# Top-k attention with two MoE layers on one core: scaling each masked tile on ScalarE in place of the product with v

## The chip, the cores and the metric

The kernel runs on one core of one Trainium2 chip. The metric is the device time of one execution in microseconds (us); lower is better. Engines are named as in the profile: PE is TensorE (matmuls and transposes), DVE is VectorE, ACT is ScalarE, POOL is GpSimd, SP is SyncE, which issues most DMAs.

## The reference

Three stages follow one another. The first is attention over 4 batches, 8 heads, 576 positions and a head size of 64, in which each row keeps only its 32 largest scores:

```python
scores = scale * np.matmul(q, k.transpose(0, 1, 3, 2))
kth = np.partition(scores, -top_k, axis=-1)[..., -top_k:-top_k + 1]
scores = np.where(scores >= kth, scores, -1000000000.0)
attn = np.exp(scores - np.max(scores, axis=-1, keepdims=True))
attn = attn / (np.sum(attn, axis=-1, keepdims=True) + 1e-09)
attn_out = np.matmul(attn, v)
```

The heads are laid side by side to 2304 tokens of 512 numbers. A dense layer follows, `(x @ w_a) * (x @ w_b) @ w_out`, with an inner width of 1536, and then a layer with 8 experts of inner width 1024, in which each token goes to the one expert with its largest gate value.

## The kernel before

**Units and tiles.** Attention goes by units: a batch `b` and a pair of heads `p`, four units to a batch, sixteen in all. The 576 queries of a unit fall into two groups, `g` = 0 with 320 and `g` = 1 with 256. A tile is 128 rows of queries of one head against all 576 keys. Group 0 has four such tiles and a fifth ("M") which holds the last 64 queries of both heads; group 1 has four. So there are nine tiles to a unit and 144 in all. Tiles of kind "N" are handled in pairs, the two heads side by side, and M alone: five steps to a unit, 80 in all.

**One pair.** PE makes the scores in two halves of keys into PSUM (L597 and L601), ACT copies each half to SBUF as `s` (L606), DVE takes elementwise maxima and minima of the halves (L614) and then, by alternating an eight-largest instruction (L625, L641, L644) and a replace instruction (L638), finds the 32nd largest value (L652). ACT computes the exponentials `e` (L633). One DVE instruction a tile (`attn_out`, L680) then compares `s` with the 32nd value, multiplies by `e`, writes the masked tile `am` and adds up its row sum in `r.sum`. PE transposes `am` in blocks of 128 (L706, L715; for M L688 to L691), ACT copies the result to `aT` (L710, L695, L717).

**One group.** When its tiles are done, `attn_av` multiplies the transposed tiles with `v` (L727, L731) and ACT copies the product, transposed and not yet divided by the row sums, to `xc` (L735). `attn_norm` makes the division: POOL adds 1e-9 to the sums (L750), DVE takes reciprocals (L752), ACT spreads each reciprocal over 64 columns in the tile `rr` (L753, L761), PE turns them into rows (L769, and for group 0 L771), and the product is multiplied by them and written to `xf`. In batches 0 and 1 ACT copies the rows to SBUF and POOL multiplies (L776, L777); in batches 2 and 3 DVE multiplies straight from PSUM (L780). POOL also writes a check value (L747).

**What follows.** `moe1(b, ...)` is the dense layer of one batch: ACT rounds `xf` to `xh` (L792), POOL subtracts the rounded part to get `xl` (L794), and PE multiplies with weights that come by DMA (L824, L854), while ACT empties PSUM (L809) and POOL multiplies and splits (L832, L400, L401). The gate of each batch ranks tokens by expert (L956 to L1011), and after the last batch eight expert steps follow (L1182, L1231). In the first quarter of the run ACT, DVE and POOL also unpack weights (L387 to L401).

**What sets the order.** The kernel writes no engine's order by hand. It registers every operation with its engine, a cost, a priority `pos` (small first) and its reads and writes, plays them through a list scheduler, and emits each engine's instructions in the order that comes out. The dense layer has a low priority on PE, so that its matmuls fill what attention leaves free. An engine then runs its own list strictly in that order. Buffers that matter here: two for the pair of masked tiles `am`, one fixed tile for M, one PSUM buffer `tp` for transposes, one PSUM buffer `pv` that the product with v, the transposed fifth block (L715) and the rows of reciprocals share, and two PSUM buffers `ab` for the dense layer.

Of the kernel before, what the change touches and what calls it, by code (L numbers as in the profile page):

```python
# [15 lines left out]
OP = mybir.AluOpType  # L16
# [176 lines left out]
def c_ts(n):  # L193
    return (n / 2 + 66) / 0.96
# [15 lines left out]
def fused_kernel(ctx: ExitStack, tc: tile.TileContext, q, k, v, w_a, w_b, w_out, w_gate, w1, w2, out,  # L210
# [43 lines left out]
    def T(pool, shape, dt, name, bufs):  # L254
        return P_.tile(pool, shape, dt, name, bufs)
# [50 lines left out]
    nc.gpsimd.memset(wg, 0.0)  # L306
    qm_t, rr_t = [], []
    for i in range(2):
        qm_t.append(cst.tile([128, 192], F32R, name=f"qm{i}"))
        nc.gpsimd.memset(fr(qm_t[i]), 0.0)  # L310
    for i in range(opts.get("rr", 1)):
        rr_t.append(cst.tile([128, 5, 128], F32, name=f"rr{i}"))
        nc.gpsimd.memset(rr_t[i], 0.0)
    id2 = cst.tile([128, 64], F32, name="id2")
    nc.vector.tensor_add(id2, idf[:, 0:64], idf[:, 64:128])
    chk_t = cst.tile([128, B * HP * 9], F32, name="chk")
# [12 lines left out]
    QM = [P_.fixed(t) for t in qm_t]  # L329
    RR = [P_.fixed(t) for t in rr_t]  # L330
    AM = [P_.fixed(t) for t in am_t]
# [138 lines left out]
    def prep_unit(u, i, pos, step):  # L470
        u.qm, u.rr = QM[i % 2], RR[i % len(RR)]
        u.qT = T(p_at, [128, 2, 512], F32R, "qT", 2)
# [73 lines left out]
    def new_group(u, g):  # L546
        r = Rec()
        r.u, r.g, r.n, r.nt = u, g, GRP[g][1], len(GT[g]) + 2
        r.kt = T(p_sml, [128, 5, 48], F32, "kt", 2)
        r.sum = T(p_sml, [128, 5], F32, "sum", 2)  # L550
        r.aT = [T(p_at, [128, 4, 320], F32, f"aT{h}", opts.get("aT", 1)) for h in range(2)]
        r.at = T(p_at, [128, 320], F32, "aTt", opts.get("aT", 1))
        r.xc = T(p_at, [128, 320], F32, "xc", opts.get("xc", 1))
        return r
# [99 lines left out]

    def attn_out(i, r, j, kind, h, c, pos, s, e):
        def kth():
            return r.kt()[:, j, 47:48]
        if kind == "M":
            amz, o, ky = AM[0], 0, None
        else:  # L660
            if not h:
                r.am = T(p_at, [128, 2 * S], F32, "am", opts.get("amb", 2))
                r.tp = T(p_ps, [128, 1024], F32, "tp", 1)
            amz, o, ky = r.am, h * S, h

        def am():
            return amz()[:, o:o + S]

        def sc():
            return s()[:, h if kind == "N" else 0]  # L670
        sk = [(s, (h, 0)), (s, (h, 1))]
        amk = (amz, ky)
        if masked(i):
            P(DVE, c_ts(S), pos, lambda: nc.vector.tensor_scalar(am(), sc(), kth(), None, op0=OP.is_ge),
              r=sk + [(r.kt, (j, 5))], w=[amk], label=f"st{i}")
            P(POOL, c_pool(S), pos, lambda: nc.gpsimd.tensor_mul(am(), am(), e()), r=[e], w=[amk])
            P(ACT, c_act(S, True) + 90, pos, lambda: nc.scalar.activation(
                e(), am(), AF.Copy, accum_out=r.sum()[:, j:j + 1]), r=[amk], w=[e, (r.sum, j)])
        else:
            P(DVE, c_dve(S) + 60, pos, lambda: nc.vector.scalar_tensor_tensor(  # L680
                am(), sc(), kth(), e(), op0=OP.is_ge, op1=OP.mult, accum_out=r.sum()[:, j:j + 1]),
              r=sk + [(r.kt, (j, 5)), e], w=[amk, (r.sum, j)], label=f"st{i}")
        if kind == "M":
            tp = T(p_ps, [128, 1024], F32, "tp", 1)
# [34 lines left out]

    def attn_av(r, pos):  # L720
        u, n = r.u, r.n
        pv = T(p_ps, [128, 512], F32, "pv", 1)

        def av():
# [9 lines left out]
          act=7.2 * n / (4 * n + 132))  # L734
        P(ACT, c_act(n), pos - 20, lambda: nc.scalar.copy(r.xc()[:, 0:n], pv()[:, 0:n]), r=[pv], w=[r.xc])  # L735

    def masked(i):

        return any(a <= i < b and i % m < n for a, b, n, m in opts.get("mk", ()))

    def b_norm(b):
        return b in opts.get("pn", (0, 1))

    def attn_norm(i, r, xf, pos):
        u, g, nt = r.u, r.g, r.nt
        c0, n = GRP[g]
        P(POOL, 170, pos, lambda: nc.gpsimd.tensor_sub(  # L747
            chk_t[:, i - nt + 1:i + 1], r.kt()[:, 0:nt, 47], r.kt()[:, 0:nt, 39]),
          r=[r.kt], w=[(CHK, i)])
        P(POOL, 180, pos - 20, lambda: nc.gpsimd.tensor_scalar(r.sum()[:, 0:nt], r.sum()[:, 0:nt], 1e-9, None, op0=OP.add),  # L750
          w=[r.sum])
        P(DVE, 100, pos - 20, lambda: nc.vector.reciprocal(r.sum()[:, 0:nt], r.sum()[:, 0:nt]), w=[r.sum])  # L752
        P(ACT, c_act(256, True), pos - 20, lambda: nc.scalar.copy(  # L753
            u.rr()[:, 2 * g:2 * g + 2, :].rearrange("p i (h d) -> p i h d", h=2),
            r.sum()[:, 0:4].rearrange("p (i h) -> p i h", h=2)[:, :, :, None].to_broadcast([128, 2, 2, 64])),
          r=[r.sum], w=[(u.rr, g)])
        if g == 0:
            def diag():
                for h in range(2):
                    p0 = 64 * h  # L760
                    res = nc.scalar.copy(u.rr()[p0:p0 + 64, 4, p0:p0 + 64],  # L761
                                         r.sum()[p0:p0 + 64, 4:5].to_broadcast([64, 64]))
                return res
            P(ACT, 300, pos - 20, diag, r=[r.sum], w=[(u.rr, 2)])
        rb = T(p_ps, [128, 512], F32, "pv", 1)

        def bc():
            for x in range(2):
                res = nc.tensor.transpose(rb()[:, x * 128:(x + 1) * 128], u.rr()[:, 2 * g + x, :], idf)  # L769
            if g == 0:  # L770
                res = nc.tensor.matmul(rb()[:, 256:320], u.rr()[:, 4, :], id2, start=True, stop=True)  # L771
            return res
        P(PE, 330 - 110 * g, pos, bc, act=0, r=[(u.rr, g)] + ([] if g else [(u.rr, 2)]), w=[rb])
        if b_norm(u.b):
            rs = T(p_at, [128, 320], F32, "rs", 1)
            P(ACT, c_act(n), pos - 20, lambda: nc.scalar.copy(rs()[:, 0:n], rb()[:, 0:n]), r=[rb], w=[rs])  # L776
            P(POOL, c_pool(n), pos, lambda: nc.gpsimd.tensor_mul(xf()[:, u.p, c0:c0 + n], r.xc()[:, 0:n], rs()[:, 0:n]),  # L777
              r=[r.xc, rs], w=[(xf, (u.p, g))], label=f"norm{u.b}{g}")
            return
        P(DVE, c_dve(n), pos - 20, lambda: nc.vector.tensor_mul(xf()[:, u.p, c0:c0 + n], r.xc()[:, 0:n], rb()[:, 0:n]),  # L780
          r=[r.xc, rb], w=[(xf, (u.p, g))], label=f"norm{u.b}{g}")

# [557 lines left out]
    for i, (ui, g, j, groups, b, p, kind, h, c) in enumerate(tiles):  # L1340
# [26 lines left out]
        for x in made:  # L1367
            attn_out(*x)
        pend = []
        if j == R.nt - 1:  # L1370
            attn_av(R, pos + 1)
            attn_norm(i, R, XF[b], pos + 2)
            if p == HP - 1 and g == groups[-1]:
                moe1(b, groups, XF[b], pos + 3)
# [211 lines left out]
```

## Time and profile before

| what | value |
|---|---|
| median of 3 runs | 1232.25 us (1228.04 to 1233.31) |
| the profiled execution, its own time | 1233.15 us |
| its span in the trace | 1231.4 us |
| mean granted TensorE clock | 0.956 of full speed |
| PE busy | 1103.6 us (90%) |
| DVE busy | 896.3 us (73%) |
| ACT busy | 718.1 us (58%) |
| POOL busy | 460.6 us (37%) |

Busy shares are means over stages with different limits, so they are to be read by stage: DVE has nearly all of its work in attention, which ends at about 810 us, PE works to the end. A matmul's end is modelled in the trace, and consecutive matmuls overlap; what one costs is the distance from its start to the next one's. The same goes for DVE and ACT, where the last part of an instruction overlaps with the next. "Idle before" is the time that an engine stood still ahead of an instruction, with what ended it.

### The profile page before, as it was taken

To read this page: it belongs to the slowest core of one execution; us is meant where nothing else is said; L and a number is where in the kernel's file an instruction comes from. 1 tells how busy PE (TensorE), PEld (TensorE's weight loads), DVE (VectorE), ACT (ScalarE), POOL (GpSimd) and SP (SyncE) were. 2 spreads that over 40 slices of the span, in tenths; PEclk is the share of its full clock that TensorE was granted. 3 is DMA by queue.
4 is the path that set the end of the run, shared out by engine and by line. 5 is a ranking of instruction groups with operands and counts; after the bars stand their busy time and mean duration, and the time that the engine had idled before them with its cause. 6 is when DMAs were issued, how large, how long until landed. Compare 5 with 4: busy or idle time off the path is not lost.

```text
span 1231.4 us, 22514 instructions
## 1 busy us (share of the span) xinstructions
PE 1103.6 (90%) x7710; PEld 981.2 (80%) x7710; DVE 896.3 (73%) x2636; ACT 718.1 (58%) x1567; POOL 460.6 (37%) x622
## 2 busy tenths in 40 slices
PE   4656796979999789999999999999999999999996
PEld 2333474868888579889888998989999899999996
DVE  6999999999998999999998999910004545444441
ACT  6667676776667567666765766633224445544551
POOL 3455566755536234234535422455234100000001
PEclk9966798989999999999999999999899999999998
DMA  8487578999677234244243442246535655554450
GB/s 235 130 276 229 164 245 261 323 303 300 208 255 248 93 87 144 109 153 144 78 152 112 132 151 104 86 155 225 191 147 184 189 152 174 176 177 151 159 177 22
DMA packets 116863, 215.49 MB, mean 175 GB/s; under 512 B 28883, under 2 KB 77011, under 8 KB 109061
## 3 DMA queue, kind: packets, MB, share of 16 engines
q1 hardware_dynamic: 113525, 204.52, 52.4%
q0 software_dynamic: 3216, 9.46, 2.0%
q8 instruction: 63, 1.03, 0.4%
q14 instruction: 59, 0.48, 0.1%
HBM read 171.82 MB, written 35.25 MB: 168 GB/s over the span
## 4 chain that ended last, share of the span: by engine, by line
PE 55%; DVE 14%; DMA 11%; issue 8%; ACT 7%; POOL 4%; SPq 1%; POOLq 0%; ACTq 0%; DVEq 0%
PE ab L824 16%; PE ab L854 9%; PE ab L1182 5%; PE pv L727 5%; DVE am L680 3%; DVE m L638 3%; PE ms L1231 3%; PE pv L1231 3%; PE sp L601 3%; DVE kt L641 2%; PE tp L706 2%; DMA xsort<-rows,pi 2%; DMA rawk<-in_k_dram 2%; DMA wt<-wos 1%; PE pv L731 1%
## 5 line engine op out<-in xcount | busy, mean ns | idle before, releaser
L824 PE MATMUL ab<-xh,wt 128*128 128x320 f32 (+1 forms) x1344 | 303.9, 304 | 3.9 <-ACT sb L809 3.8
L824 PEld LDWEIGHTS ab<-xh,wt 128*128 128x128 f32 x1344 | 227.6, 191 | 13.2 <-issue 7.8
L824 PE MATMUL ab<-xl,wt 128*128 128x320 f32 (+1 forms) x672 | 199.9, 297 | 0.0
L638 DVE MATCH_REPLACE8 m<-kt,m 128x288 f32<-128x288 f32 x432 | 188.5, 440 | 0.0
L641 DVE MAX8 kt<-m 128x8 f32<-128x288 f32 x432 | 182.3, 444 | 0.5
L854 PE MATMUL ab<-gH,wt 128*128 128x320 f32 (+1 forms) x768 | 171.8, 305 | 4.5 <-DMA wt<-wos 4.5
L680 DVE SCALAR_TENSOR_TENSOR am<-s,kt,e 128x576 f32<-128x576 f32 x144 | 139.8, 996 | 0.3
L854 PEld LDWEIGHTS ab<-gH,wt 128*128 128x128 f32 x768 | 130.7, 193 | 6.7 <-DMA wt<-wos 3.9
L832 POOL TENSOR_TENSOR sa<-sa,sb 128x320 f32<-128x320 f32 (+1 forms) x96 | 79.6, 829 | 145.0 <-ACT sb L809 144.5
L824 PEld LDWEIGHTS ab<-xl,wt 128*128 128x128 f32 x672 | 128.8, 192 | 0.0
L633 ACT ACTIVATE e<-s,nm 128x576 f32<-128x576 f32 x144 | 108.6, 778 | 11.6 <-POOL nm L628 11.3
L854 PE MATMUL ab<-gT,wt 128*128 128x320 f32 (+1 forms) x384 | 115.1, 300 | 0.0
L1256 POOL DMA_INDIRECT out_dram<-y,ti x23 | 23.0, 999 | 227.6 <-ACT y L1250 212.6
L1100 DVE TENSOR_TENSOR wp<-raw,wp 128x1024 fp32r<-128x1024 f32 (+1 forms) x73 | 67.4, 942 | 55.6 <-ACT wp L1099 55.2
L606 ACT COPY s<-sp 128x576 f32<-128x576 f32 x128 | 81.9, 640 | 42.9 <-PE sp L601 23.7
L706 PE MATMUL tp<-idr,am 128*128 128x128 f32 x512 | 84.8, 304 | 20.3 <-ACT aT L710 7.2
L401 POOL TENSOR_TENSOR gT<-sa,gH 128x320 fp32r<-128x320 f32 (+1 forms) x96 | 84.6, 881 | 45.8 <-ACT gH L400 45.4
L706 PEld LDWEIGHTS tp<-idr,am 128*128 128x128 f32 x512 | 64.1, 155 | 38.6 <-ACT aT L710 15.8
L1182 PE MATMUL ab<-xgh,wp 128*128 128x304 f32 (+6 forms) x352 | 89.4, 312 | 1.1 <-DVE gT L1189 0.7
L710 ACT COPY aT<-tp 128x512 f32<-128x512 f32 x128 | 72.4, 587 | 26.6 <-PE tp L706 25.8
L727 PE MATMUL pv<-aT,vt 128*64 128x320 f32 (+1 forms) x512 | 79.2, 451 | 6.5 <-ACT aT L695 4.5
L809 ACT ACTIVATE sa<-ab 128x320 f32<-128x320 f32 (+1 forms) x120 | 49.4, 412 | 53.9 <-PE ab L824 30.7
(303 smaller groups left out, 2560.8 us busy)
## 6 DMA issues: line engine op xcount, KB each, us to landing
wt<-ws SPq DMA_DIRECT2D x54, 1024.0 KB, 5.6
wt<-wos SPq DMA_DIRECT2D x44, 768.0 KB, 5.7
raw<-in_moe_w_dram SPq DMA_DIRECT2D x64, 512.0 KB, 3.7
kS<-kT SPq DMA_DIRECT2D x24, 304.0 KB, 4.5
xsort<-rows SPq DMA_DIRECT2D x8, 771.0 KB, 14.4
wp<-ws SPq DMA_DIRECT2D x6, 1024.0 KB
vt<-in_v_dram SPq DMA_DIRECT2D x20, 256.0 KB, 3.1
gT<-in_moe_w_a_dram SPq DMA_DIRECT2D x8, 512.0 KB, 4.1
```

The source lines that it names most:

```text
L401: P(POOL, c_pool(cost), pos, lambda: nc.gpsimd.tensor_sub(lo(), src(), fr(hi())), r=rd + wh, w=wl)
L606: P(ACT, c_act(S), pos, lambda hf=hf, sp=sp: nc.scalar.copy(s()[:, :, hf * HS:(hf + 1) * HS], sp()[:, :, 0:HS]), r=[sp], w=[(s, (h, hf)) f ...
L633: P(ACT, c_act(S, True) + 90, pos, lambda h=h, e=e: nc.scalar.activation(e(), s()[:, h], AF.Exp, bias=nm()[:, h], scale=SCALE), r=[(s, (h, ...
L638: P(DVE, c_dve(HS), pos + 5.0 * h, lambda x=x, h=h, j=j: nc.vector.match_replace(out=m()[:, h], in_to_replace=kt(j, 8 * x - 8, 8 * x), in_ ...
L641: P(DVE, c_dve(HS), pos + 5.0 * h, lambda x=x, h=h, j=j: nc.vector.max(out=kt(j, 8 * x, 8 * x + 8), in_=m()[:, h]), r=[(m, h)], w=[KT(j, x)])
L680: P(DVE, c_dve(S) + 60, pos, lambda: nc.vector.scalar_tensor_tensor(am(), sc(), kth(), e(), op0=OP.is_ge, op1=OP.mult, accum_out=r.sum()[: ...
L706: res = nc.tensor.transpose(tp()[:, 512 * h + x * 128:512 * h + (x + 1) * 128], z()[:, 640 * h + x * 128:640 * h + (x + 1) * 128], idf)
L727: nc.tensor.matmul(pv()[64 * h:64 * h + 64, 0:n], u.vt()[:, h, j, :], r.aT[h]()[:, j, 0:n], start=(j == 0), stop=False)
L824: res = nc.tensor.matmul(pa()[:, 0:n], view()[:, m, wi, ko, :], xv()[:, ko], start=(ko == 0 and x == 0), stop=(ko == KO - 1 and x == 2))
L832: P(POOL, c_pool(n), pos, lambda: nc.gpsimd.tensor_mul(sa()[:, 0:n], sa()[:, 0:n], sb()[:, 0:n]), r=[sb], w=[sa])
L854: res = nc.tensor.matmul(pa()[:, 0:n], wv()[:, wi, f, :], gv()[:, f, :], start=(f == 0 and x == 0), stop=(f == HB - 1 and x == 2))
L1182: res = nc.tensor.matmul(pa()[:, 0:cap], p1[ko]()[:, wi, f * 128:(f + 1) * 128], xv()[:, ko], start=(ko == 0 and i == 0), stop=(ko == KO - ...
```

## The change

ACT divides each masked tile by its row sum before the transposes, so that the product with v is already divided. After a pair's (or M's) comparisons, `attn_div` has DVE add 1e-9 to the sums and take reciprocals: two small instructions a step, 80 times each. `attn_out` is split: part 0 is the comparison, part 1 begins with an ACT copy of the 576 columns of `am` in place with the reciprocal as its scale, and goes on with the transposes as before. ACT's copy behind the product with v now writes `xf` and not `xc`. What falls away: the sum on POOL, the reciprocals by group, `rr` and its copies, the turning into rows on PE with its small matrices, the copy of the rows, the products on POOL and DVE. The check value stays. The branch `masked` that is deleted was never taken. No DMA is added, removed or moved.

```diff
+    def attn_div(r, j0, j1, pos):
+        w = [(r.sum, j) for j in range(j0, j1)]
+        P(DVE, 70, pos, lambda: nc.vector.tensor_scalar(r.sum()[:, j0:j1], r.sum()[:, j0:j1], 1e-9, None, op0=OP.add), w=w)
+        P(DVE, 80, pos, lambda: nc.vector.reciprocal(r.sum()[:, j0:j1], r.sum()[:, j0:j1]), w=w)
...
-    def attn_out(i, r, j, kind, h, c, pos, s, e):
+    def attn_out(part, i, r, j, kind, h, c, pos, s, e):
...
-        else:
+        if part == 0:
             P(DVE, c_dve(S) + 60, pos, lambda: nc.vector.scalar_tensor_tensor(
                 am(), sc(), kth(), e(), op0=OP.is_ge, op1=OP.mult, accum_out=r.sum()[:, j:j + 1]),
               r=sk + [(r.kt, (j, 5)), e], w=[amk, (r.sum, j)], label=f"st{i}")
+            return
+        P(ACT, c_act(S, True) + 30, pos, lambda: nc.scalar.activation(
+            am(), am(), AF.Copy, scale=r.sum()[:, j:j + 1]), r=[(r.sum, j)], w=[amk])
...
-        P(ACT, c_act(n), pos - 20, lambda: nc.scalar.copy(r.xc()[:, 0:n], pv()[:, 0:n]), r=[pv], w=[r.xc])
+        P(ACT, c_act(n), pos - 20, lambda: nc.scalar.copy(xf()[:, u.p, c0:c0 + n], pv()[:, 0:n]), r=[pv],
+          w=[(xf, (u.p, r.g))], label=f"norm{u.b}{r.g}")
...
-    def attn_norm(i, r, xf, pos):
+    def attn_check(i, r, pos):
...
-        P(POOL, 180, pos - 20, lambda: nc.gpsimd.tensor_scalar(r.sum()[:, 0:nt], r.sum()[:, 0:nt], 1e-9, None, op0=OP.add),
-          w=[r.sum])
-        P(DVE, 100, pos - 20, lambda: nc.vector.reciprocal(r.sum()[:, 0:nt], r.sum()[:, 0:nt]), w=[r.sum])
...
-        for x in made:
-            attn_out(*x)
+        for x in made:
+            attn_out(0, *x)
+        attn_div(R, j + 1 - len(pend), j + 1, made[-1][6])
+        for x in made:
+            attn_out(1, *x)
```

## Rows read from the trace of the kernel before

**Rows 1.** Busy time in three stretches (us and count, by engine):
```profile
0.00:437.80 437.80, 339.06 (x2154) 265.78 (x2155) 411.25 (x1251) 300.45 (x653) 229.21 (x295) 0.90 0.74 231
437.80:825.40 387.60, 377.98 (x2876) 343.25 (x2874) 342.44 (x1098) 247.78 (x574) 153.84 (x226) 1.00 0.38 123
825.40:1231.40 406.00, 386.54 (x2688) 372.18 (x2684) 142.64 (x288) 169.86 (x340) 77.51 (x103) 0.98 0.50 164
```

**Rows 2.** All engines in order of time, end of batch 1 (start, length, us):
```profile
433.55 0.37 ACT L735 COPY xc<-pv 128x256 f32<-128x256 f32 x1 [1.95 <-PE pv L731]
...
435.31 0.73 POOL L777 TENSOR_TENSOR xf<-xc,rs 128x256 f32<-128x256 f32 x1 [7.03 <-ACT rs L776]
...
437.83 0.35 PE L824 MATMUL ab<-xh,wt 128*128 128x256 f32 x1
```

**Rows 3.** POOL in order of time, end of batch 3's attention:
```profile
812.29 0.74 POOL L794 TENSOR_TENSOR xl<-xf,xh 128x256 fp32r<-128x256 f32 x1 [0.86 <-ACT xh L792]
```

**Rows 4.** PE in order of time, first matmul of batch 3's dense layer:
```profile
825.36 0.41 PE L824 MATMUL ab<-xh,wt 128*128 128x320 f32 x1
```

**Rows 5.** DVE's waits up to 437.8 us (total, times, longest):
```profile
DVE m L614 <- ACT s L606: 7.0, 6, 3.4
DVE sum L752 <- POOL sum L750: 5.1, 6, 2.3
DVE n L614 <- ACT s L606: 3.3, 6, 0.7
```

**Rows 6.** Groups by line (busy us, mean ns | idle before):
```profile
L633 ACT ACTIVATE e<-s,nm 128x576 f32<-128x576 f32 x144 | 108.6, 778 | 11.6 <-POOL nm L628 11.3
...
L1250 ACT ACTIVATE y<-sp,xr 128x512 f32<-128x512 f32 (+6 forms) x19 | 12.4, 683 | 5.7 <-issue 2.6 <-PE sp L1301 1.8 <-PE sp L1273 0.9
...
L1028 ACT COPY rows<-ms 128x512 f32<-128x512 f32 (+1 forms) x16 | 9.4, 586 | 11.3 <-DMA xsort<-rows,pi 10.2 <-PE ms L1025 1.1
...
L753 ACT COPY rr<-sum 128x256 f32<-128x256 f32 x32 | 12.9, 404 | 5.0 <-DVE sum L752 4.8
...
L777 POOL TENSOR_TENSOR xf<-xc,rs 128x320 f32<-128x320 f32 (+1 forms) x16 | 16.0, 999 | 20.3 <-ACT rs L776 20.3
```

**Rows 7.** ACT in order of time, two exponentials back to back:
```profile
452.56 1.44 ACT L633 ACTIVATE e<-s,nm 128x576 f32<-128x576 f32 x2 [0.50 <-POOL nm L628]
```

**Rows 8.** DVE in order of time, small instructions of the gate:
```profile
645.98 0.80 DVE L970 TENSOR_TENSOR gb<-gb,iom 128x40 f32<-128x40 f32 x1
...
647.93 0.19 DVE L998 TENSOR_SCALAR gb<-gb 128x5 f32<-128x5 f32 x1
648.04 0.44 DVE L644 MAX8 kt<-n 128x8 f32<-128x288 f32 x1
648.41 0.16 DVE L1000 RECIPROCAL gb<-gb 128x5 f32<-128x5 f32 x1
648.50 0.71 DVE L614 TENSOR_TENSOR m<-sp,s 128x576 f32<-128x576 f32 x1
```

**Rows 9.** The same instructions with nothing between them:
```profile
932.33 0.17 DVE L998 TENSOR_SCALAR gb<-gb 128x3 f32<-128x3 f32 x1
932.60 0.18 DVE L1000 RECIPROCAL gb<-gb 128x3 f32<-128x3 f32 x1
```

**Rows 10.** POOL in order of time, at the first row of rows 8:
```profile
645.84 0.87 POOL L401 TENSOR_TENSOR gT<-sa,gH 128x320 fp32r<-128x320 f32 x1 [0.89 <-ACT gH L400]
```

**Rows 11.** Instructions of line 389 (shortest, median, longest ns):
```profile
L389 DVE TENSOR_SCALAR gH<-gH x10: 400/410/1522, 10.8 to 223.9; 128x512 int32<-128x512 int32 x10
```

**Rows 12.** DVE busy with line 680 alone, up to 437.8 us:
```profile
0.00:437.80 437.80, 74.46 (x148) 0.90 0.74 231
```

**Rows 13.** PE in order of time, turning reciprocals into rows:
```profile
456.96 0.38 PE L769 MATMUL pv<-idr,rr 128*128 128x128 f32 x2
457.18 0.33 PE L771 MATMUL pv<-id,rr 128*128 128x64 f32 x2
457.32 0.36 PE L824 MATMUL ab<-xh,wt 128*128 128x256 f32 x1
```

More of the change, by code (lines that the diff above doesn't have):

```diff
@@ L306, in fused_kernel @@
     nc.gpsimd.memset(wg, 0.0)
-    qm_t, rr_t = [], []
+    qm_t = []
     for i in range(2):
@@ L310, in fused_kernel @@
         nc.gpsimd.memset(fr(qm_t[i]), 0.0)
[L311 to L315, printed above, removed]
     chk_t = cst.tile([128, B * HP * 9], F32, name="chk")
@@ L329, in fused_kernel @@
     QM = [P_.fixed(t) for t in qm_t]
-    RR = [P_.fixed(t) for t in rr_t]
     AM = [P_.fixed(t) for t in am_t]
@@ L470, in prep_unit @@
     def prep_unit(u, i, pos, step):
-        u.qm, u.rr = QM[i % 2], RR[i % len(RR)]
+        u.qm = QM[i % 2]
         u.qT = T(p_at, [128, 2, 512], F32R, "qT", 2)
@@ L552, in new_group @@
         r.at = T(p_at, [128, 320], F32, "aTt", opts.get("aT", 1))
-        r.xc = T(p_at, [128, 320], F32, "xc", opts.get("xc", 1))
         return r
@@ L660, in attn_out @@
         else:
-            if not h:
+            if part == 0 and not h:
                 r.am = T(p_at, [128, 2 * S], F32, "am", opts.get("amb", 2))
+            if part and not h:
                 r.tp = T(p_ps, [128, 1024], F32, "tp", 1)
@@ L672, in attn_out @@
         amk = (amz, ky)
[L673 to L678, printed above, removed]
-        else:
+        if part == 0:
             P(DVE, c_dve(S) + 60, pos, lambda: nc.vector.scalar_tensor_tensor(
@@ L718, in attn_out, with attn_av @@
               w=[(r.at, o2)], label="aT")
-    def attn_av(r, pos):
-        u, n = r.u, r.n
+    def attn_av(r, xf, pos):
+        u, n, c0 = r.u, r.n, GRP[r.g][0]
         pv = T(p_ps, [128, 512], F32, "pv", 1)
@@ L734, in attn_av @@
           act=7.2 * n / (4 * n + 132))
-        P(ACT, c_act(n), pos - 20, lambda: nc.scalar.copy(r.xc()[:, 0:n], pv()[:, 0:n]), r=[pv], w=[r.xc])
[L737 to L742, printed above, removed]
-    def attn_norm(i, r, xf, pos):
-        u, g, nt = r.u, r.g, r.nt
-        c0, n = GRP[g]
+        P(ACT, c_act(n), pos - 20, lambda: nc.scalar.copy(xf()[:, u.p, c0:c0 + n], pv()[:, 0:n]), r=[pv],
+          w=[(xf, (u.p, r.g))], label=f"norm{u.b}{r.g}")
+    def attn_check(i, r, pos):
+        nt = r.nt
         P(POOL, 170, pos, lambda: nc.gpsimd.tensor_sub(
@@ L749, in attn_norm @@
           r=[r.kt], w=[(CHK, i)])
-        P(POOL, 180, pos - 20, lambda: nc.gpsimd.tensor_scalar(r.sum()[:, 0:nt], r.sum()[:, 0:nt], 1e-9, None, op0=OP.add),
-          w=[r.sum])
-        P(DVE, 100, pos - 20, lambda: nc.vector.reciprocal(r.sum()[:, 0:nt], r.sum()[:, 0:nt]), w=[r.sum])
[L753 to L781, printed above, removed]
     def moe1(b, groups, xf, pos):
@@ L1367, in fused_kernel @@
         for x in made:
-            attn_out(*x)
+            attn_out(0, *x)
+        attn_div(R, j + 1 - len(pend), j + 1, made[-1][6])
+        for x in made:
+            attn_out(1, *x)
         pend = []
         if j == R.nt - 1:
-            attn_av(R, pos + 1)
-            attn_norm(i, R, XF[b], pos + 2)
+            attn_av(R, XF[b], pos + 1)
+            attn_check(i, R, pos + 2)
             if p == HP - 1 and g == groups[-1]:
```

## The prediction

> **What bounds the kernel now.** I looked first at the busy time of each engine, cut where PE takes up a new batch of the dense layer [rows 1]. Up to 437.8 us DVE is busy 411.3 of 437.8 us and PE 339.1. From there to 825.4 PE is busy 378.0 of 387.6 and DVE 342.4; after that PE is busy 386.5 of 406.0 and DVE 142.6. So the first stretch is DVE's and all that follows is PE's.
>
> The second view, all engines in order of time, shows how the two join. The product of batch 1's last group reaches SBUF at 433.55, is multiplied by its reciprocals at 435.31, and PE begins batch 1's dense layer at 437.83 [rows 2]. The end of attention in batches 0 and 1 thus sets when PE gets its long work, and from there PE idles only 9.6 us to 825.4. At the end of batch 3's attention it is the other way round: POOL has the last part of `xl` at 812.29 + 0.74 = 813.0 [rows 3], and PE takes it up at 825.36 [rows 4]. Attention is there 12.3 us early, which hides any loss on DVE behind 437.8 that is smaller than that, and any gain.
>
> The third view, DVE's waits in the first stretch, shows what could be won there: 7.0 + 3.3 us for the score copies of ACT and 5.1 us for POOL's addition to the sums [rows 5].
>
> So the sum has two parts: what DVE needs more or less up to 437.8, and what PE needs more or less after it. What ACT does counts only where it makes one of the two wait.
>
> **The change part by part, up to 437.8 us** (batches 0 and 1: 8 units, 40 steps, 16 groups).
>
> *The two small DVE instructions.* The gate of the dense layer runs the same pair. With another instruction between, the addition is followed after 648.04 - 647.93 = 0.11 us and the reciprocal after 648.50 - 648.41 = 0.09 [rows 8]: 0.20 a step. With nothing between, the reciprocal starts 932.60 - 932.33 = 0.27 us behind the addition [rows 9]; if the addition waits as long for the row sum, the step costs 0.27 + 0.27 + 0.09 = 0.63. Next to the comparison DVE mostly has work of the following pair, so I take 0.20: 40 x 0.20 = **+8.0 us**, up to 40 x 0.63 = 25.
>
> *What leaves DVE.* 16 reciprocals by group at 0.09 are -1.4 us. The wait for POOL's addition goes with it, -5.1 [rows 5]: the addition is DVE's own now. Both together **-6.5**.
>
> *What leaves POOL.* 16 products, 16.0 us [rows 6]. A DVE instruction with two inputs in SBUF stands still while POOL works: 128x40 took 0.80 us at 645.98, and ended with a POOL instruction that ran from 645.84 to 646.71 [rows 8, 10], where a neighbour of a few columns took 0.19. The comparison takes 74.5 of the 437.8 us, 17% [rows 12]; 17% of 16.0 is 2.7 us of overlap, at the mean half of it lost: **-1.4**, between 0 and -2.7.
>
> *Is the new addition held by POOL too?* It has one input in SBUF. With 512 columns such an addition has a median of 410 ns and took up to 1522 [rows 11]; with 5 columns it took 190 ns, but beside a POOL instruction as short as itself [rows 8]. So the bounds are 0 and all additions held. Without its products POOL is busy (229.2 - 16.0) / 437.8 = 49% of the stretch, in instructions of 229.2 / 295 = 0.78 us on average [rows 1]; an addition that comes at any time waits 0.49 x 0.39 = 0.19 us, 40 of them 7.6. I take half, **+3.8**, since the rows lie on either side.
>
> The Trainium skill, "SBUF — State Buffer", section "SBUF: two separate sides", states that VectorE and GpSimd share one pair of ports, held for a whole instruction by whoever comes first, and that on VectorE's side instructions in a two-port mode or with two SBUF inputs take part. The 0.80 us at 645.98 agrees. By the rule, an addition of few columns is held if it runs in that mode, and the term would be 7.6 in place of 3.8; no row here shows which.
>
> *ACT's scaling.* An exponential of the same 576 columns, with one per-partition operand, takes 778 ns; a per-partition scale on another copy lengthens it from 586 to 683 [rows 6], so the scaling should also last 0.78. Two exponentials in a row take 1.44 us [rows 7], so the next instruction starts after 1.44 - 0.78 = 0.66. For the 74 tiles of this stretch that is 49 us. What leaves ACT, 16 spreads of 0.40 = 6.5 us [rows 6] and some smaller copies, I leave at 6.5. ACT goes from 300.5 to 343 us busy, 69% to 78%: no bound, but a fuller queue. Behind a scaling that waits for DVE's reciprocal stand the score copies, and DVE waits for those: 10.3 us now [rows 5]. Idle time on ACT falls from 31% to 22%; if waits rose as 31/22, that would be +4.2. Some of the 8.0 us of new work falls into those very waits, so I take **+2.0**, between -10.3 (all gone, because the group's closing work has left the queue) and +10.
>
> *The step's length.* Before PE can transpose there now stand an addition, a reciprocal and a scaling, 0.20 + 0.78, and 0.66 more for the second head: 1.6 us. At the group's end the way from the product's copy to `xf` shrinks from 435.31 + 0.73 - 433.55 = 2.5 us to that copy itself, 0.37 [rows 2]: 2.1 less. The two nearly cancel where batch 1 ends; I count **0**, -2 to +2. Inside a batch the longer step is covered by the next pair, whose masked tile has a buffer of its own.
>
> Sum to 437.8: 8.0 - 6.5 - 1.4 + 3.8 + 2.0 = **+5.9 us**.
>
> **From 437.8 on.** For group 0, PE gave 457.32 - 456.96 = 0.36 us to the rows, of which the two transposes 0.22 [rows 13]; group 1 has only those. Batches 2 and 3: 8 x 0.36 + 8 x 0.22 = **-4.6 us** on the engine that bounds. Against it, PE's queue now waits for ACT's scaled tile where it waited for DVE's tile. It idles 9.6 us in all in this stretch [rows 1]. Two copies of that sort wait in one queue now, and ACT's busy share goes from 64% to (247.8 + 46 - 6.5) / 387.6 = 74%; I take **+2.0**, from 0 to 14 (below). On DVE, eight units gain and lose as above and lose the products as well; the 12.3 us of lead [rows 3, 4] cover it, and without them 8.0 + 3.8 us would show here too. The stretch behind 825.4 is not touched.
>
> **Total.** 5.9 - 4.6 + 2.0 = +3.3 us on the profiled execution, which took 1233.15 us (span 1231.4, 1.75 around it). The median lies 0.9 below it: 1232.25 + 3.3 = **1235.5**.
>
> **The rivals.** All times stand against the median.
>
> *PE waits for the scaled tile.* For it speaks that PE executes strictly in its list's order, with dense-layer work behind the transposes; against it, that it loses so little now. If each of the 40 steps after 437.8 held PE for half a scaling's distance, 0.35 us, that is 14 in place of 2: 1247.5. It passes 0.5% from about 0.12 us a step. Chance 0.15.
>
> *DVE's small steps stand bare.* If nothing is ready between comparison, addition and reciprocal, the 8.0 becomes 25: 1252.7. Against it speaks that DVE was idle for only 26 us in the first stretch, so work was mostly at hand. Chance 0.06.
>
> *Every addition is held by POOL*, 7.6 for 3.8 (the mechanism of the two-port rule above): 1239.3. Chance 0.10. The skill's page named there gives no more than that condition.
>
> *The group's closing work was what made DVE wait*, the one that ends faster. Before, two copies on ACT, transposes on PE and a product stand at each group's end in the same queues as the next pair's score copies. If the 10.3 us of waits vanish with them, in place of +2.0, the sum is 3.3 - 12.3 = -9.0: 1223.2. For it: these waits are few and long, up to 3.4 us [rows 5], as of something out of the usual beat. Against it: ACT gets seven times more work than it loses. It decides once about 9.5 of the 12.3 are had. Chance 0.20.
>
> **How the numbers follow.** About 0.5% (6.2 us) is what a measurement of this kernel can tell from no change. The forecast's own case, 1229 to 1242, has 0.49; about a sixth of it, 0.08, lies above 1238.4. Slower: 0.15 + 0.06 + 0.10 + 0.08 = 0.39, of which 0.02 stays within since PE's wait may be below 0.12; 0.37. Faster: 0.20, less 0.02 for a partial gain, 0.18. The rest, 0.45, is within 0.5%. The range leaves out the bare steps and the far halves of the PE and closing-work cases, 0.2 in all: 1222 to 1249.
>
> **What the profile after would show.** Up to the start of batch 1's dense layer: line 824 should resume at about 437.8 + 6 = 444 us; if it resumes before 434, the closing-work case holds. Two small DVE instructions 80 times, followed after 0.1 us each; a longest addition near 0.9 us would mean that POOL holds it, below 0.25 that it does not. The scaling near 0.78 us, ACT busy 75 to 80% in attention. No rows from reciprocals on PE. PE idle between the start of batch 1's and of batch 3's dense layer near 12 us; 20 or more speaks for the first rival. Wrong would be the whole frame if PE stood idle behind 825, or if attention's end passed PE's leftover work, so that PE waited for batch 3.

## The result, and the profile after

The changed kernel takes **1248.51 us** (median of 4 runs, 1247.71 to 1251.51) against 1232.78 us for the kernel before in the same comparison: ratio 1.0125, 95% interval 1.0097 to 1.0154, some 15 us slower. The forecast was 1235.5; the measured time lies at the upper end of the range, which ends at 1249. The profiled execution took 1247.71 us, with a span of 1245.7.

The busy times by stretch of the changed kernel, cut at the same two marks as [rows 1] (there 437.8 and 825.4: PE's first dense-layer matmul of batch 1's second group, and of batch 3):

```profile
core 0: us, PE busy (x) PEld busy (x) DVE busy (x) ACT busy (x) POOL busy (x), PEclk, DMA share, GB/s
0.00:467.80 467.80, 348.09 (x2103) 271.13 (x2104) 430.19 (x1324) 332.83 (x676) 206.34 (x262) 0.85 0.69 216
467.80:845.20 377.40, 369.75 (x2829) 336.77 (x2829) 342.64 (x1137) 281.60 (x616) 153.46 (x210) 1.00 0.39 127
845.20:1245.70 400.50, 383.32 (x2688) 368.50 (x2684) 142.57 (x288) 169.48 (x340) 77.36 (x103) 0.99 0.50 166
```

The first stretch is 30.0 us longer, the second 10.2 shorter, the third 5.5 shorter; together +14.3, the difference of the spans. The frame held: DVE sets the first stretch, PE the others. In the first, DVE is busy for 18.9 us more and idle for 11.0 us more (467.8 - 430.2 = 37.6, before 26.6). These two numbers are what has to be explained.

For the busy time, the groups of DVE instructions of the first stretch in the changed kernel, shapes apart (busy, mean ns):

```profile
L674 DVE SCALAR_TENSOR_TENSOR am<-s,kt,e 128x576 f32<-128x576 f32 x74 | 71.9, 991 | 2.0 <-ACT e L626 1.8
L651 DVE TENSOR_SCALAR sum<-sum 128x2 f32<-128x2 f32 x33 | 16.5, 500 | 0.1
L652 DVE RECIPROCAL sum<-sum 128x2 f32<-128x2 f32 x33 | 4.9, 148 | 0.1
L652 DVE RECIPROCAL sum<-sum 128x1 f32<-128x1 f32 x8 | 1.2, 152 | 0.0
L651 DVE TENSOR_SCALAR sum<-sum 128x1 f32<-128x1 f32 x8 | 1.1, 141 | 0.0
```

An addition of one column takes 141 ns, one of two columns 500 on average. The order of time shows why; two of the longest, each beside the POOL instruction under way:

```profile
212.03 1.36 POOL L395 TENSOR_TENSOR gH<-gH 128x512 fp32r<-128x512 f32 x1 [0.73 <-ACT gH L394]
212.18 1.22 DVE L651 TENSOR_SCALAR sum<-sum 128x2 f32<-128x2 f32 x1
...
417.01 1.44 POOL L508 TENSOR_TENSOR hl<-rawq,hl 128x576 fp32r<-128x576 f32 x1 [1.47 <-ACT hl L506]
417.19 1.28 DVE L651 TENSOR_SCALAR sum<-sum 128x2 f32<-128x2 f32 x1
```

POOL ends at 213.39 and 418.45, the additions at 213.40 and 418.47: each stood until POOL was done. Of the 33 additions of two columns in this stretch, 19 began while such a POOL instruction ran and ended 0.02 to 0.03 us behind it; the other 14 took 0.14 to 0.17 us. The addition is held, for a time that has nothing to do with its 256 elements. The Trainium skill has the condition on two pages: "SBUF — State Buffer", section "SBUF: two separate sides", says that a VectorE instruction in a two-port mode waits for a GpSimd instruction that came first, and "VectorE: DVE Perf Modes", section "What auto-detection actually checks", gives as the condition of the mode a single source and the destination in SBUF, with outermost dimensions other than one that are both even or equal. The trace agrees with both: two columns are held, one column is not.

For the idle time, DVE's waits up to 467.8 (us in total, times, longest), to be held against [rows 5]:

```profile
DVE m L607 <- ACT s L599: 14.3, 5, 7.6
DVE gT L383 <- ACT gT L381: 7.2, 1, 7.2
DVE m L607 <- PE sp L594: 5.1, 1, 5.1
DVE n L607 <- ACT s L599: 4.7, 7, 0.8
DVE am L674 <- ACT e L626: 1.8, 2, 1.2
...
DVE m L606 <- ACT s L577: 1.5, 2, 1.1
```

The wait for POOL's sum is gone, and in its place stand longer waits for scores and their copies, most of it in three places: 5.14 us at 244.35, 3.39 at 322.42 and 7.61 at 381.57. All engines in order of time around the longest:

```profile
375.48 0.58 PE L782 MATMUL ab<-xh,wt 128*128 128x256 f32 x1 [3.45 <-DMA wt<-ws]
...
379.70 0.44 PE L594 MATMUL sp<-kT,qT 128*128 128x288 f32 x1
...
380.90 0.64 ACT L599 COPY s<-sp 128x576 f32<-128x576 f32 x1 [1.64 <-PE sp L594]
...
381.57 0.76 DVE L607 TENSOR_TENSOR m<-sp,s 128x576 f32<-128x576 f32 x1 [7.61 <-ACT s L599]
```

No wait for the division is in this chain. PE's list has dense-layer matmuls of batch 0 ahead of the second half of a score. Their weights came late (why was not looked into), PE stood for 3.45 us, and behind the pause it was granted 0.50 of its clock (1.2 GHz) from 375.4 to 380.6; from there to 390 the mean was 0.97. The matmuls in it started 0.21 us apart, not 0.12. Only then came the score, and DVE stood for 7.61 us. That the order of the lists had a part in the loss is what the experiments then had to test, beside the addition and ACT's load.

### The profile page after: what moved, and what is told of

The parts are those of the page before. It is cut to its first block, busy times and chain, and to the rows that moved or that the text cites. A ratio compares the mean times of both kernels' runs of the same rounds, so it can differ in the third digit from the quotient of the medians.

```text
span 1245.7 us, 22374 instructions
## 1 busy us (share of the span) xinstructions
PE 1101.2 (88%) x7614; PEld 976.4 (78%) x7614; DVE 915.4 (73%) x2747; ACT 783.9 (63%) x1631; POOL 437.2 (35%) x573
## 4 chain that ended last, share of the span: by engine, by line
PE 44%; DVE 10%; ACT 7%; issue 7%; DMA 7%; POOL 2%; SPq 0%; POOLq 0%; ACTq 0%; DVEq 0%
PE ab L782 12%; PE ab L812 9%; PE ab L1140 4%; PE ms L1189 3%; PE pv L1189 3%; PE pv L724 2%; DMA xsort<-rows,pi 2%; PE sp L594 2%; PE tp L703 2%; DVE m L631 2%; DVE am L674 2%; DVE kt L634 2%; DMA wt<-wos 1%; ACT am L678 1%; ACT aT L707 1%
## 5 line engine op out<-in xcount | busy, mean ns | idle before, releaser
L790 POOL TENSOR_TENSOR sa<-sa,sb 128x320 f32<-128x320 f32 (+1 forms) x96 | 84.1, 876 | 146.4 <-ACT sb L767 144.2
L678 ACT ACTIVATE am<-am,sum 128x576 f32<-128x576 f32 x144 | 107.4, 773 | 21.8 <-DVE sum L652 21.7
L703 PE MATMUL tp<-idr,am 128*128 128x128 f32 x512 | 81.3, 301 | 27.4 <-ACT am L678 13.0
L703 PEld LDWEIGHTS tp<-idr,am 128*128 128x128 f32 x512 | 64.3, 154 | 43.3 <-ACT am L678 23.7
L724 PE MATMUL pv<-aT,vt 128*64 128x320 f32 (+1 forms) x512 | 80.3, 458 | 4.5 <-ACT aTt L714 2.2
```

The costliest lines, as they stand in the source:

```text
L678: P(ACT, c_act(S, True) + 30, pos, lambda: nc.scalar.activation(am(), am(), AF.Copy, scale=r.sum()[:, j:j + 1]), r=[(r.sum, j)], w=[amk])
L703: res = nc.tensor.transpose(tp()[:, 512 * h + x * 128:512 * h + (x + 1) * 128], z()[:, 640 * h + x * 128:640 * h + (x + 1) * 128], idf)
L724: nc.tensor.matmul(pv()[64 * h:64 * h + 64, 0:n], u.vt()[:, h, j, :], r.aT[h]()[:, j, 0:n], start=(j == 0), stop=False)
L790: P(POOL, c_pool(n), pos, lambda: nc.gpsimd.tensor_mul(sa()[:, 0:n], sa()[:, 0:n], sb()[:, 0:n]), r=[sb], w=[sa])
```

## The experiments

The marks are the two of the table of stretches; "idle" is DVE's idle time in the first. Ratios stand against the kernel before, measured beside each kernel, with their 95% interval. Stretches and idle times are those of the one profiled execution, which lies up to 3.3 us off the median of its kernel (e1 3.1 us above, e3 3.3 below); differences of a few us between two kernels' stretches are therefore not shown by them alone.

| kernel | median us | ratio | first, second, third stretch | idle |
|---|---|---|---|---|
| before | 1232.25 | 1 | 437.8, 387.6, 406.0 | 26.6 |
| changed | 1248.51 | 1.0125 (1.0097 to 1.0154) | 467.8, 377.4, 400.5 | 37.6 |
| e1, no addition | 1237.6 | 1.0040 (1.0020 to 1.0060) | 457.1, 376.1, 405.8 | 41.0 |
| e2, addition by column | 1238.74 | 1.0051 (1.0029 to 1.0074) | 458.1, 376.3, 405.1 | 39.4 |
| e3, no scaling | 1229.76 | 0.9986 (0.9968 to 1.0004) | 446.8, 371.7, 405.9 | 23.7 |
| e4, no division | 1226.8 | 0.9956 (0.9937 to 0.9976) | 444.6, 371.5, 406.3 | 34.5 |
| e10, scaled aside, no addition | 1235.02 | 1.0013 (0.9997 to 1.0030) | 449.0, 375.8, 407.1 | 36.3 |
| e11, one column scaled, no addition | 1225.32 | 0.9927 (0.9905 to 0.9950) | 445.4, 370.7, 407.2 | 34.3 |
| e7, no division, own lists | 1216.21 | 0.9860 (0.9834 to 0.9886) | 435.9, 370.4, 406.3 | 29.3 |
| e12, no addition, own lists | 1220.8 | 0.9886 (0.9863 to 0.9910) | 440.5, 373.9, 404.8 | 28.3 |
| e14, before in other lists | 1232.25 | 0.9998 (0.9979 to 1.0016) | 440.6, 385.9, 406.3 | 30.6 |
| e6, before without POOL's addition | 1230.59 | 0.9980 (0.9963 to 0.9997) | 435.0, 387.6, 403.8 | 22.5 |
| e9, both ways in one | 1215.16 | 0.9852 (0.9831 to 0.9873) | 437.2, 372.5, 404.6 | 24.8 |
| e13, the division in e7's lists | 1318.88 | 1.0682 (1.0650 to 1.0713) | 484.0, 428.1, 405.3 | 67.0 |

In e1 to e4, e6, e10 and e11 an operation keeps its place in the scheduler but issues something else or nothing, so that every engine's order stays as it was.

**e1: the addition left out, same lists.**

```diff
-        P(DVE, 70, pos, lambda: nc.vector.tensor_scalar(r.sum()[:, j0:j1], ...), w=w)
+        P(DVE, 70, pos, lambda: None, w=w)
```

> The changed kernel without the addition of 1e-9 (left out; reciprocal, scaling and the order of everything else stay). Theory A, POOL holds the addition: its 64 instances of two columns last 0.38 us on average, 17.6 us of DVE's time in the first stretch, and DVE bounds that stretch. Then batch 1's dense layer resumes near 468 - 16 = 452 us and the time falls to 1231 to 1237. Theory B, ACT's fuller queue sets the pace (DVE's waits for score copies rose by some 11 us) and the addition stands in waits that are there anyway: the dense layer resumes at 463 or later, 1244 to 1248.

The time fell by 0.85%, some 10.5 us, and the dense layer resumed at 457.1: between the two theories, nearer to A. DVE is busy for 14.1 us less in the stretch (416.1 for 430.2), but idle for 3.4 more, since the three long waits stay:

```profile
234.62 0.76 DVE L607 TENSOR_TENSOR m<-sp,s 128x576 f32<-128x576 f32 x1 [4.08 <-PE sp L594]
...
313.89 0.76 DVE L607 TENSOR_TENSOR m<-sp,s 128x576 f32<-128x576 f32 x1 [3.70 <-ACT s L599]
...
373.35 0.76 DVE L607 TENSOR_TENSOR m<-sp,s 128x576 f32<-128x576 f32 x1 [8.57 <-ACT s L599]
```

**e2: the same additions, column by column.**

```diff
-    lambda: nc.vector.tensor_scalar(r.sum()[:, j0:j1], r.sum()[:, j0:j1], 1e-9, None, op0=OP.add)
+    lambda: [nc.vector.tensor_scalar(r.sum()[:, x:x + 1], r.sum()[:, x:x + 1], 1e-9, None, op0=OP.add)
+             for x in range(j0, j1)][-1]
```

> The changed kernel with each addition of two columns issued as two additions of one column; nothing is left out. In the changed kernel's trace none of the 16 additions of one column lasted over 0.17 us. Theory A, the hold by POOL comes with the second column: 144 additions of about 0.14 us, none over 0.25; some 0.2 us a pair are had back, 6 to 9 us in the first stretch, 1239 to 1243. Rival, every small instruction that depends on the one before it costs this much whatever its width: two of them cost more than one, 1250 to 1256, and additions over 0.5 us are still there.

Theory A, though 1238.74 lies just below its 1239 to 1243. All 144 additions last between 125 and 154 ns, though 70 of them ran from start to end beside a POOL instruction (at 97.32, for one, in an instruction from 96.37 to 98.17):

```profile
L651 DVE TENSOR_SCALAR sum<-sum 128x1 f32<-128x1 f32 x144 | 15.4, 139 | 0.0
```

The time is within the error of e1's, so nearly all that the addition costs is the hold, and it goes with the second column.

**e3 and e4: without the scaling, and without any division.**

```diff
-            am(), am(), AF.Copy, scale=r.sum()[:, j:j + 1]), r=[(r.sum, j)], w=[amk])
+        P(ACT, c_act(S, True) + 30, pos, lambda: None, r=[(r.sum, j)], w=[amk])
```

(e4 leaves out addition and reciprocal in the same way.)

> The changed kernel without ACT's scaling (the tiles stay undivided; addition and reciprocal are still made, but nobody reads their result). Theory A: the scaling costs what DVE's waits for score copies grew by and the longer step, 8 to 13 us, 1236 to 1241, and the additions stay as long as before. Theory B: with the scaling all of the loss in the first stretch goes, 1226 to 1233.

> The changed kernel without addition, reciprocal and scaling (nothing is divided). What is left of the change is then only what it removes. Sum of theory A: 17.6 of additions, some 5 of reciprocals and 11 of waits leave the first stretch: dense layer of batch 1 at about 468 - 34 = 434, and the time 1213 to 1219 where attention's lead lets it, not below the 1216 that PE's part behind it needs by more than a few us. If what the change removes was what made DVE wait, the dense layer resumes well before 434, at 425 or less.

e3 gave back 1.39%, 17 us: more than theory A has, within what theory B has. e4 should have been the sum of both savings and isn't: it lies only 3 us below e3. And it fails the other way too: with nothing of the division left, and without the old closing work, the dense layer resumes at 444.6, later than before. DVE does no more work there than before (410.1 us busy, before 411.3) but idles for 34.5 us in place of 26.6, and the long waits stand where they stood in the changed kernel:

```profile
233.05 0.76 DVE L607 TENSOR_TENSOR m<-sp,s 128x576 f32<-128x576 f32 x1 [3.92 <-ACT gH L394]
...
309.09 0.76 DVE L607 TENSOR_TENSOR m<-sp,s 128x576 f32<-128x576 f32 x1 [3.86 <-ACT s L599]
...
363.77 0.76 DVE L607 TENSOR_TENSOR m<-sp,s 128x576 f32<-128x576 f32 x1 [7.27 <-ACT s L599]
```

So something is left that neither theory had. What e4 still shares with the changed kernel is the order of its lists; e7 and e12 test that.

**e10 and e11: ACT's load without PE's wait, and the wait without the load** (both without the addition, so they stand against e1).

```diff
-            am(), am(), AF.Copy, scale=...
+            scr[:, 0:S], am(), AF.Copy, scale=...                        # e10
+            am()[:, 0:1], am()[:, 0:1], AF.Copy, scale=...               # e11
```

> The changed kernel without the addition, and with ACT writing the scaled tile into a scratch tile that nobody reads: ACT does the same work at the same places, but PE's transposes take DVE's unscaled tile and no longer wait for ACT (the output stays undivided). To be held against the run without the addition (1237.6, dense layer at 457.1). Theory queue, the scaling costs by filling ACT's queue ahead of the score copies: it stays at 1235 to 1238. Theory step, it costs by PE's queue, where scores and dense-layer work stand behind transposes that wait for the scaled tile: 1227 to 1231, and PE's 18.5 us of waits for the scaled tile in the first stretch are gone.

> The changed kernel without the addition, and with ACT scaling only the first of the 576 columns of each tile: PE still waits for ACT at each tile, but ACT has about 0.55 us less to do for each (the output stays undivided but for that column). Theory queue: nearly all of what leaving the scaling out gave back comes back, 1228 to 1231. Theory step: PE still waits for ACT to come round to the instruction; half or less comes back, 1232 to 1236.

The queue theory in both, and e11 lies even below the range that the theory gave. With the whole load and no wait of PE for the scaled tile, 1.0013, just below e1's interval, though the two intervals overlap. With the wait (PE still stands 12.7 us for the tile in the stretch, 18.5 in e1) and a scaling of 291 ns, 0.9927, no slower than without any division. In these lists ACT's time is most of what the scaling costs. What PE's wait adds is less certain: 2.6 us by the medians, but the profiled execution of e10 has a first stretch 8.1 us shorter than e1's. Where the load is gone, nothing of it is seen.

```profile
L678 ACT ACTIVATE am<-am,sum 128x1 f32<-128x1 f32 x74 | 19.6, 291 | 11.8 <-DVE sum L652 11.5
```

**e7 and e12: the same instructions in lists of their own.** e7 is e4 and e12 is e1, with what they leave out taken from the scheduler as well, so that it plans anew.

```diff
-        P(DVE, 70, pos, lambda: nc.vector.tensor_scalar(...), w=w)       # e12; in e7 also attn_div and the scaling
```

> The changed kernel without addition, reciprocal and scaling (nothing is divided), and with the instruction lists planned for that: the run without the division kept the lists that were planned with them. Theory order: there DVE still had three long waits at the places of the changed kernel (3.9, 3.9 and 7.3 us), since the lists place dense-layer work of batch 0 ahead of scores; with lists of its own the long waits are elsewhere or gone, batch 1's dense layer resumes at 430 to 436 instead of 444.6, and the time is 1215 to 1222. Rival, the order weighs nothing and the rest is in the instructions themselves: 1225 to 1229, and waits of the same sum.

> The changed kernel without the addition, as in the first experiment, but with the lists planned without it too; all other instructions are the same. Theory, the list's long waits are chance and not the division's: the time differs from 1237.6 by 5 us or more, in either direction, and DVE's waits of over 3 us stand elsewhere or are gone. Rival, any list that has the scaling in it must put the scores late: 1235 to 1240, with the three waits of 4 to 8 us.

The largest effect of all. e7 is 0.96% below e4, e12 1.54% below e1 (medians 10.6 and 16.8 us apart), and neither executes anything else than its partner. e12 against e1 in the first stretch, by busy time and DVE's waits:

```profile
0.00:440.50 440.50, 335.38 (x2103) 263.44 (x2104) 412.21 (x1263) 329.65 (x673) 207.10 (x260) 0.86 0.72 229
```

The waits of e1, then those of e12:

```profile
DVE m L607 <- ACT s L599: 15.8, 5, 8.6
...
DVE n L607 <- ACT s L599: 5.3, 7, 1.1
DVE m L607 <- PE sp L594: 4.1, 1, 4.1
DVE m L606 <- ACT s L577: 3.5, 2, 2.2
```

```profile
DVE m L607 <- ACT s L599: 6.9, 7, 3.2
DVE n L607 <- ACT s L599: 5.7, 7, 1.1
DVE m L607 <- PE sp L594: 5.6, 2, 5.4
```

The stretch ends 16.6 us sooner. DVE idles for 28.3 us, not 41.0; its waits for scores and their copies fall from 28.7 to 18.2. Of the three long waits two are left, 3.17 and 5.41 us; in e7 too two (4.83 and 3.51): a list of its own took away one of the three and shortened the longest. The rival to e12 (any list with the scaling in it puts the scores late, 1235 to 1240) is refuted. Between e7 and e12, with and without reciprocals and scaling and each in its own list, lie 1220.8 - 1216.2 = 4.6 us, 3.2 by the ratios, whose intervals overlap; between e4 and e1 in one list they are 10.8. Since the lists differ as well, 4.6 is not the price of these instructions alone.

**e13: the division put into e7's lists.** Reciprocals by head and the scaling are issued where the transposes were planned to start, with PE, POOL and SP in e7's order.

> The division executed (reciprocals by head, scaling; no addition) in the lists that were planned without it: on PE, POOL and SP the same order as in the replanned run without division (1216.2), and on DVE and ACT the new instructions are put in where the transposes were planned to start. The fourth of a set of four: with the changed kernel's list 1226.8 without and 1237.6 with the division. If list and division add up, 1225 to 1229. If the list without room for the scaling makes PE wait for each scaled tile, 1232 or more, with PE waiting over 30 us for them in the first stretch.

1318.88 us (ratio 1.0682, 1.0650 to 1.0713). In 17 of the 64 pairs the transposed fifth block is taken ahead of the second head's scaling, so some columns stay undivided; the instructions are all there. List and division don't add up. PE's waits in the first stretch, here up to 484:

```profile
PE tp L707 <- ACT am L680: 62.2, 52, 2.9
PE tp L688 <- ACT am L680: 18.1, 8, 5.3
```

In a list that has no room for the scaling PE stands 80.3 us for scaled tiles in the first stretch and 45.1 in the second, where e12 has 14.8 and 1.3; the time is 98 us above e12, which makes the same division in a list planned with it. The order must be planned with the scaling; it is then a question of which of such lists comes out.

**e14: the kernel before in other lists.**

```diff
-        P(POOL, 180, pos - 20, lambda: nc.gpsimd.tensor_scalar(r.sum()[:, 0:nt], ...
+        P(POOL, 230, pos - 20, lambda: nc.gpsimd.tensor_scalar(r.sum()[:, 0:nt], ...
```

> The kernel before with the same instructions, all of them, and lists planned with 230 in place of 180 ns for POOL's addition: only the order differs (1132 lines of PE's list). If the size of what a list does by chance is as large as what was seen between the two runs without division (10 us), it should show here: 1227 or less or 1240 or more. Rival, the lists planned from the same costs are about alike: 1230 to 1237.

The rival: the same time, ratio 0.9998. A new list doesn't have to cost anything: in the profiled execution the first stretch ran 2.8 us longer and the second 1.7 shorter.

**e6: before without POOL's addition**, lists kept.

```diff
+        P(POOL, 180, pos - 20, lambda: None,
```

> The kernel before without POOL's addition to the sums (1e-9 is not added), its lists kept. DVE waited 5.1 us for that addition in the first stretch, and the prediction counted these as gained. Theory, the wait is worth what it lasts: the first stretch shrinks by 4 to 5 us, 1228 to 1230. Rival, the time only moves into DVE's next wait for a score copy: within 1.5 us of before, 1232 to 1235, with about 5 us more of those waits.

Between the two: 2.5 us of the 5.1 (0.20%, 0.03 to 0.37). In the profiled execution DVE idles for 4.1 us less, and part of the wait moves to the score copies (8.6 and 3.7 us here, 7.0 and 3.3 in [rows 5]):

```profile
DVE m L614 <- ACT s L606: 8.6, 7, 3.9
DVE gT L389 <- ACT gT L387: 6.9, 1, 6.9
DVE n L614 <- ACT s L606: 3.7, 6, 0.7
```

**e9: both ways in one kernel.** The division as before in batches 0 and 1, the scaled tile in 2 and 3, no addition anywhere (a row's sum holds an exponential of zero, so it is at least about 1, and 1e-9 doesn't show beside that in this number format).

```diff
+        if scaled(r.u.b):                                  # batches 2 and 3
+            P(ACT, c_act(S, True) + 30, pos, lambda: nc.scalar.activation(
+                am(), am(), AF.Copy, scale=r.sum()[:, j:j + 1]), r=[(r.sum, j)], w=[amk])
```

> Both ways of dividing in one kernel: batches 0 and 1 as in the kernel before (reciprocals turned into rows, product scaled), but without POOL's addition; batches 2 and 3 with the scaled tile as in the changed kernel, but without DVE's addition; 1e-9 is added nowhere. The changed kernel lost 30 us in the first stretch and gained 10 us in the second, which PE bounds. If these belong to the stretches, the first takes about 433 (5 us of waits for POOL gone), the second 376 to 378, the last 402 to 406: 1213 to 1220. Rival: attention of batch 3, whose lead of 12.3 us the shorter second stretch uses up, becomes the bound: the second stretch stays at 383 or more and the time at 1222 to 1229. A list planned anew can move either by several us.

1215.16 us, 1.5% below the kernel before (1.3 to 1.7%), and the fastest of all that make the division. By busy time in its three stretches:

```profile
0.00:437.20 437.20, 337.39 (x2154) 263.90 (x2155) 412.37 (x1249) 300.89 (x653) 226.89 (x279) 0.90 0.74 232
437.20:809.70 372.50, 368.07 (x2828) 336.75 (x2826) 339.59 (x1108) 281.00 (x614) 153.51 (x210) 1.00 0.39 128
809.70:1214.30 404.60, 385.90 (x2688) 371.51 (x2684) 142.46 (x288) 169.11 (x340) 77.66 (x103) 0.98 0.49 164
```

The first stretch did not fall to 433 (437.2, as before); the second fell by more than expected, to 372.5. The rival's bound did not come: the last part of `xl` is there at 803.57 + 0.74 = 804.3, still 5.4 us ahead of PE.

## Why the prediction was right or wrong

**The frame** was right: DVE bounds the first stretch, PE the rest, and the loss is in the first and a gain in the second. That the time lies inside the range is luck all the same: it is 13.0 us above the forecast and 0.5 below the upper end, and that end was set by the case that PE waits for scaled tiles (1247.5), which did not come behind the first stretch. One correction: 437.83 was not the first matmul of batch 1's dense layer. 24 of group 0 ran from 416.96; at 437.83 group 1 comes in and the work runs on.

**The step that failed** is "I take +2.0" for DVE's waits on ACT's queue, with +10 as its upper bound. Waits for scores, their copies and the exponentials went from 11.4 us (7.0 + 3.3 in [rows 5], and 1.1 for PE, in the line below) to 27.4 (14.3 + 5.1 + 4.7 + 1.8 + 1.5), +16.0.

```profile
DVE m L614 <- PE sp L601: 1.1, 2, 0.7
```

The working scaled old waits by ACT's idle share, as if the order stood still. No term allowed for a new list, though the scheduler plans all of them anew for a changed kernel. e12 against e1 shows that the list made most of it: with the same instructions, all of the division but the addition, those waits are 18.2 us and not 30.7 (28.7 and 2.0 for exponentials), and the time is 16.8 lower.

**The held addition**, +3.8, was the right mechanism and mis-sized: 33 x (0.500 - 0.141) = 11.8 us in the stretch, over the 7.6 that the prediction gave for all of them held. That bound took POOL's mean instruction, 0.78 us, and half of it as the wait; but a moment drawn at random falls more often into a long one (1.36 and 1.44 us in the rows above, up to 1.83 beside other additions). Weighted by length, half an instruction of POOL in this stretch is 0.57 us and not 0.39. That gives 33 x 0.44 x 0.57 = 8.3 us by estimate; beyond it, 19 of the 33 met POOL at work, where its busy share of 44% would make it 15. Why more of them did was not looked into. By e1 the addition as a whole is worth some 10 us of the total, by e2 its hold some 9. The rival *every addition is held by POOL* was thus true in its mechanism, except for the single-column ones, and not in its 1239.3.

**The two small instructions**, +8.0: right in kind, too high. In the changed kernel an addition that isn't held is followed after 0.05 to 0.07 us and a reciprocal after 0.06 to 0.08, so a step costs some 0.13 us, not 0.20, and the 41 steps of the stretch some 5.4. They do not stand bare. Column by column the additions cost 1 us of the time over none at all, which is within the error. Of DVE's 18.9 us more of busy time, counted from each start to the next, the additions with their hold take 14.4 and the reciprocals 2.9; old reciprocals (1.6) and shorter comparisons go off, and some 5 us, spread over many lines, are not traced.

**What leaves DVE**, -6.5: e6 gives 2.5 for the 5.1 of the wait. A wait in front of a bounding engine is not worth its length if the next one begins where it ended.

**POOL's products**, -1.4: the comparisons fell from 74.0 to 71.9 us, -2.1, inside the bounds. So is **the step's length**, 0: from batch 1's last comparison to the mark it was 437.83 - 425.94 = 11.9 us before and is 467.81 - 454.07 = 13.7, +1.8. One scaling lasts 0.77 us, as forecast.

**PE's rows**, -4.6: too small. PE's busy time in the second stretch fell by 8.2 (378.0 to 369.75), 8.8 in e12; the starts of neighbours, by which I priced them, missed nearly half. **PE's wait for the scaled tile**, +2.0 there: did not come. PE's wait for it is 0.7 us in that stretch, and its idle time fell from 9.6 to 7.6. The rival *PE waits for the scaled tile* holds nowhere behind the first stretch. So -2.6 forecast, -10.2 measured, and -13.7 and -15.1 in e12 and e9. The 12.3 us of lead covered DVE's losses there: the last part of `xl` came at 842.28 + 0.74 = 843.0, 2.2 us ahead of PE's 845.17. The lead is 2.2 us in e1 and e4 too, where DVE has less to do, so it is these lists and not DVE's load that shortened it.

**The group's closing work** as the cause of DVE's waits: refuted as told, since work resumed at 467.8 and not before 434. The removal is worth much all the same: e7, which only removes, is 1.4% faster than the kernel before, most of it in the second stretch (387.6 to 370.4).

**The third stretch**, counted as untouched, took 400.5 us in this one execution and 403.8 to 407.2 in the thirteen others of the table, e4 with the same lists among them. The trace shows where its -5.5 comes from: shorter pauses, and a clock that did not fall. In the kernel before PE stood for 3.77 us up to 864.06 and for 2.89 up to 958.01, and its granted clock was 0.90 from 851.4 to 884.1 and 0.94 from 939.0 to 968.6. In the changed kernel's execution the pauses at the same places were 1.41 and 2.42 us long and the clock was 1.00 in both stretches, and the same matmuls took 28.4 and 27.3 us, not 32.7 and 29.6. In e1 and e4, with the changed kernel's lists, the first of these stretches has 0.89 and 0.95 and the second 0.94. So it belongs to this execution and not to the change; why the pauses were shorter is open.

**What stays open.** Why the scheduler's list for the changed kernel was that much worse. It may be chance: three pairs of lists with the same instructions differ by 16.8, 10.6 and 0.6 us, which are too few to say. Nor was it separated how much of the later scores is PE's clock, whose mean over the first stretch is 0.90 before and 0.85 after. The complete change, addition and all, in a better list was not run; from e12 and the 10.5 us of e1 I would estimate 1231, about where the kernel before stands.

## What to carry to other kernels

Where a scheduler writes the order, an edit changes two things, the instructions and the lists: run the new instructions in the old order, or the old places with nothing in them, before blaming an instruction, and plan more than once before judging an edit. Put a small VectorE instruction that works beside GpSimd into a form that isn't held (one column, or none, where the constant doesn't matter). And place an edit by the stretch whose bound it relieves: the scaled tile paid where PE is the limit (10 to 15 us in the second stretch) and won nothing where DVE is and ACT feeds it (the first stretch is 2.7 us longer in e12 and 30.0 in the changed kernel).

## What was not expected of the hardware

An fp32 addition of two columns waits for POOL's instruction to its end (0.50 us on average in the first stretch, 1.28 at most, ending 0.02 to 0.03 us behind POOL's); of one column it never does (125 to 154 ns in 144 cases). One of two columns that began 0.39 us into a POOL instruction that only issues a DMA (L992, 0.98 us from 677.87) took 0.15 us and was not held. And a pause of 3.45 us on PE, for weights, was followed by 5.2 us at 0.50 of the clock, in which the dense layer's matmuls started 0.21 us apart in place of 0.12; that put off a score by some 2 us beyond the pause itself.
